# Linear attention followed by a SiLU feed-forward on one Trainium2 core: loads and work units in another order, and query and key transposes by DMA for two thirds of the chunks

## The chip, the cores and the metric

The kernel runs on one core of one Trainium2 chip. Times are microseconds (us) on the device, of the slowest (here the only) core. The span that a profile gives is from the first to the last instruction of the profiled execution and is about 2 us less than the device time of that run.

PE is TensorE (PEld its weight loads, which overlap), DVE is VectorE, ACT is ScalarE, POOL is GpSimd. SP is the SyncE queue, which here issues nearly every DMA, in program order.

## The reference, cut to what matters

```python
# q, k, v: (4 batches, 8 heads, 768 positions, 64), float32; decay lam per head
for b in range(nb):                        # blocks of 64 positions
    intra = einsum(q_b, k_b) * Dmask       # lam ** (i - j) for i >= j, else 0
    out_b = intra @ v_b + (q_b * lam ** (pos + 1)) @ kv_state
    kv_state = lam ** 64 * kv_state + (k_b * lam ** (63 - pos)).T @ v_b
x = out rearranged to (3072 tokens, 512)
h = x @ w_in                               # (512, 2048)
y = (h * sigmoid(h)) @ w_out               # (2048, 512)
```

## The kernel before

It takes 24 chunks of 128 positions (six for each of four batches), all eight heads at once. For each chunk: three loads of 256 KB (q, k, v), scaling of q and k to bf16 on POOL (`prep`), eight TensorE transposes that DVE copies out of psum, the memory that matmuls write to (`st_t`), a state product (`st_d`), scores times the causal mask (`st_s`), and the output, which already comes out transposed for the feed-forward (`st_o`). Queries go to a block-diagonal tile `qbd`, whose other half is zero, so that two heads share a matmul. Chunks are put together to groups of 512 or 256 tokens. A group then has 16 up-projections (`ffn1`, four matmuls each, SiLU on ACT) and, for each chunk, four down-projection units (`ffn2`, four matmuls each).

The program order on each engine is the order in which these functions are called. The parts that matter here:

```python
GROUPS = [512, 256, 256, 512, 512, 512, 512]

def prep(c):
    ...
    nc.gpsimd.tensor_tensor(qb, qf, lam_fwd[...], op=AL.mult)
    nc.gpsimd.tensor_tensor(kb, kf, lam_bwd[...], op=AL.mult)
    nc.scalar.activation(vb, vf, AF.Copy)          # the value cast

def st_t(c):
    tp = psum.tile([128, 2, NP, BLK], BF16, tag="att", bufs=3)
    for p in range(NP):
        nc.tensor.transpose(tp[:, 0, p, :], pair_of(qb, p), ident)
    for p in range(NP):
        nc.tensor.transpose(tp[:, 1, p, :], pair_of(kb, p), ident)
    nc.vector.tensor_copy(qt[0:64, :, 0, :], tp[0:64, 0, :, :])
    nc.vector.tensor_copy(qt[64:128, :, 1, :], tp[64:128, 0, :, :])
    nc.vector.tensor_copy(kt, tp[:, 1, :, :])
...
# start: four chunks, then the first group's up-projections
for c in range(1, n0):
    if c + 1 < n0:
        prep(c + 1)
    st_t(c), st_d(c)
    st_o(c - 1)
    st_s(c)
st_o(n0 - 1)
cast_w("in", 0)
...
for m in range(16):
    ffn1(0, m)
    ...                                            # casts and loads of weights
for i in range(4):
    cast_w("out", i)                               # four casts on DVE, in a row
...
for g in range(1, len(GROUPS)):
    while done_c < cst[g] + nch[g]:                # one attention piece,
        next_att()                                 # one down-projection unit
        next_down(g)
    for m in range(16):
        ffn1(g, m)
        next_down(g)
        ...                                        # attention pieces of the next group
```

## Time and profile before

The time is 257.65 us (median of 4 runs, 256.52 to 258.14).

From the page of the profile, in order: the span; busy time of each engine, its share and its instructions; and three rows with one digit for each of 40 equal slices of the span (6.4 us each): busy tenths of TensorE, granted TensorE clock in tenths (the part of full speed that the throttle allowed), busy tenths of the 16 DMA engines.

```profile
span 254.6 us, 3566 instructions
...
PE 221.1 (87%) x1353; PEld 124.9 (49%) x1376; DVE 102.0 (40%) x177; ACT 112.9 (44%) x238; POOL 51.1 (20%) x57
...
PE   0756994269998899899998999998999999999994
...
PEclk9999999559999999999999999999999999999998
DMA  6999899999999766945397011101101110111122
```

TensorE is at 9 nearly everywhere from slice 9 on, but there is a dip in slices 6 to 8 (38 to 57 us), where the clock falls too, and a slow start up to slice 3 (25 us).

Busy time flatters TensorE, because matmuls overlap. A better measure is pure work: the number of weight loads in a stretch (there is one for each matmul, and none is missing from the trace) times the time from one matmul's start to the next in dense places. Read from the timeline at full clock: 0.216 us for 512 columns (4 in 0.86), 0.163 for 384 (4 in 0.65), 0.109 for 256, 0.056 for a transpose or another 128-column matmul. What a stretch is longer than its work, TensorE lost. This "lost time" is used all through this text.

| stretch, us | work | lost |
|---|---|---|
| 0 to 23.5 | 7.2 | 16.3 |
| 23.5 to 48.5 | 16.7 | 8.3 |
| 48.5 to 80 | 23.5 | 8.0 |
| 80 to 100 | 18.7 | 1.3 |
| 100 to 180 | 76.0 | 4.0 |
| 180 to 254.6 | 69.5 | 5.1 |
| sum | 211.5 | 43.1 |

Three of these stretches in the windows view. The columns are the window, its length, then busy us (and instructions) of PE, PEld, DVE, ACT and POOL, the granted clock, the DMA share and GB/s. (The DMA share is the time that packets took over 16 engines; it goes above 1 where they overlap.)

```profile
23.50:48.50 25.00, 18.30 (x89) 8.11 (x88) 8.02 (x8) 13.41 (x23) 4.17 (x4) 0.93 0.97 296
48.50:80.00 31.50, 25.89 (x172) 16.60 (x176) 15.04 (x27) 10.78 (x28) 9.73 (x10) 0.84 1.17 231
...
100.00:180.00 80.00, 76.93 (x494) 44.03 (x501) 36.56 (x68) 43.23 (x93) 21.83 (x21) 1.00 0.44 89
```

The clock of 0.93 and 0.84 in the first two rows is part of their loss. The Trainium skill ("TensorE: Matmul & The Clock Gate", Part 1) says that TensorE falls to half its clock after an idle window of about 3.4 us and needs as much sustained activity to come back. The trace agrees on the fall and roughly on the return: after the gaps shown next (5.3 and 4.8 us), the four 512-column matmuls at 53.99 us start 0.43 us apart, twice 0.216, full pace is back at about 58.5 us, some 5 us after work resumed at 53.16, and the mean clock from 50 to 60 us is 0.58.

The hole itself, in the timeline view (start, duration, engine, line, operation, output and inputs, count, and in brackets the idle time just before it and what ended that):

```profile
40.74 0.38 PE L173 MATMUL kv_ps<-vb,kb 128*128 128x128 bf16 x4
...
45.17 1.23 DVE L112 CAST w_out_bf<-t 128x2048 bf16<-128x2048 f32 x1 [9.41 <-DMA t<-in_moe_w_out_dram]
46.45 1.86 PE L235 MATMUL o_ps<-w_out_bf,g 128*128 128x512 bf16 x4 [5.33 <-DVE w_out_bf L112]
...
50.67 1.23 DVE L112 CAST w_out_bf<-t 128x2048 bf16<-128x2048 f32 x1 [1.57 <-DMA t<-in_moe_w_out_dram]
...
51.81 0.41 DVE L159 COPY qbd_101<-tp 64x512 bf16<-64x512 bf16 x1
...
53.16 1.03 PE L186 MATMUL sp<-qbd_101,kt 128*128 128x256 bf16 x4 [4.84 <-DVE kt L161]
```

TensorE finishes chunk 4's state product at 41.1 us and then has almost nothing. DVE waits 9.4 us for the second out-weight, casts three out-weights one after another as they come, and only then, at 51.81, copies chunk 4's transposes, which had been in psum since 40 us. So chunk 4's scores start at 53.16.

The transposes, in the groups view (count, busy us and mean ns of one, idle before and what ended it). Keys have a second group of the same size:

```profile
L154 PE MATMUL tp<-ident,qb 128*128 128x128 bf16 x96 | 9.7, 227 | 8.3 <-POOL qb L142 6.8 <-DVE ss L189 1.6
```

A transpose lasts 227 ns, but the next starts 56 ns later, so the 192 of them are 10.7 us of TensorE's work.

### The profile page before, as it was taken

The numbers are of one execution on the slowest core, as the hardware profiler recorded it, in microseconds if no ns is written. First come the engines' busy times: TensorE is split into PE (matmuls) and PEld (weight loads), VectorE is DVE, ScalarE is ACT, GpSimd is POOL, SyncE is SP. The second block draws the span as 40 slices with busy tenths as digits, with TensorE's granted clock in tenths as the row PEclk, the third lists the DMA queues.
The fourth block names the chain that finished last, engine by engine and source line by source line (L and its number), as shares of the span: only waits on it lengthen the run. The fifth ranks groups of instructions, "written<-read, shape, count | busy, mean of one in ns | idle before, by whom it ended". The sixth has DMA issues, their size and how long they took to land.

```text
span 254.6 us, 3566 instructions
## 1 busy us (share of the span) xinstructions
PE 221.1 (87%) x1353; PEld 124.9 (49%) x1376; DVE 102.0 (40%) x177; ACT 112.9 (44%) x238; POOL 51.1 (20%) x57
## 2 busy tenths in 40 slices
PE   0756994269998899899998999998999999999994
PEld 0534442035567667555565555554555544444441
DVE  2678410464345457434463534453353430111221
ACT  4146774003428455736585356535535543333000
POOL 3650033063113333331242231132000000000000
PEclk9999999559999999999999999999999999999998
DMA  6999899999999766945397011101101110111122
GB/s 132 220 259 374 290 232 290 337 221 217 195 269 272 164 148 140 221 74 127 84 230 138 0 41 45 41 1 44 41 0 44 41 41 0 44 41 41 41 85 82
DMA packets 82721, 33.79 MB, mean 133 GB/s; under 512 B 75536, under 2 KB 75536, under 8 KB 82704
## 3 DMA queue, kind: packets, MB, share of 16 engines
q1 hardware_dynamic: 82560, 33.56, 56.3%
q8 instruction: 11, 0.18, 0.3%
q14 instruction: 6, 0.05, 0.1%
q10 hardware_dynamic: 144, 0.00, 0.0%
HBM read 27.27 MB, written 6.29 MB: 132 GB/s over the span
## 4 chain that ended last, share of the span: by engine, by line
PE 73%; DVE 7%; DMA 6%; ACT 5%; SPq 5%; issue 2%; POOL 1%
PE o_ps L235 32%; PE hp L221 25%; DMA t<-in_moe_w_out_dram 5%; PE sp L186 4%; PE op L206 3%; PE op L209 3%; PE tp L156 2%; DVE ss L189 2%; SPq L133 2%; ACT xt L212 2%; PE tp L154 2%; ACT xt L211 2%; PE kv_ps L173 2%; SPq L132 1%; DMA lam_sb<-in_lam_dram 1%
## 5 line engine op out<-in xcount | busy, mean ns | idle before, releaser
L221 PE MATMUL hp<-xt,w_in_bf 128*128 128x512 bf16 (+1 forms) x433 | 98.0, 347 | 6.0 <-ACT xt L212 3.4
L235 PE MATMUL o_ps<-w_out_bf,g 128*128 128x512 bf16 x376 | 96.4, 385 | 5.9 <-DVE w_out_bf L112 5.3
L224 ACT ACTIVATE g<-hp 128x512 bf16<-128x512 f32 (+1 forms) x112 | 59.7, 537 | 80.1 <-PE hp L221 78.4
L235 PEld LDWEIGHTS <-g 128*128 128x128 bf16 x384 | 38.0, 99 | 46.9 <-issue 7.1
L221 PEld LDWEIGHTS <-w_in_bf 128*128 128x128 bf16 x448 | 42.4, 98 | 37.0 <-issue 7.7
L142 POOL TENSOR_TENSOR qb<-qf,lam_fwd 128x512 bf16<-128x512 f32 x24 | 25.0, 1044 | 113.8 <-PE tp L154 76.0
L189 DVE TENSOR_TENSOR ss<-sp,mask 128x512 bf16<-128x512 f32 x48 | 31.1, 686 | 21.4 <-PE sp L186 21.2
L239 DVE COPY ob<-o_ps 128x512 f32<-128x512 f32 x24 | 16.6, 692 | 53.0 <-PE o_ps L235 53.0
L211 ACT ACTIVATE xt<-op 64x256 bf16<-64x256 f32 x48 | 18.1, 377 | 31.6 <-PE op L209 29.4
L143 POOL TENSOR_TENSOR kb<-kf,lam_bwd 128x512 bf16<-128x512 f32 x24 | 25.0, 1043 | 12.7 <-PE kv_ps L173 10.5
L206 PE MATMUL op<-ss,vb 128*128 128x256 bf16 x96 | 22.4, 284 | 0.9 <-DVE ss L189 0.6
L144 ACT ACTIVATE vb<-vf 128x512 bf16<-128x512 f32 x24 | 15.0, 625 | 9.1 <-DMA vf<-in_v_dram 9.0
L212 ACT ACTIVATE xt<-op 64x256 bf16<-64x256 f32 x48 | 18.2, 380 | 0.6
L154 PE MATMUL tp<-ident,qb 128*128 128x128 bf16 x96 | 9.7, 227 | 8.3 <-POOL qb L142 6.8
L186 PEld LDWEIGHTS <-kt 128*128 128x128 bf16 x96 | 9.1, 101 | 16.0 <-DVE kt L161 9.6
L176 DVE CAST kvs<-kv_ps 128x512 bf16<-128x512 f32 x20 | 13.7, 687 | 6.2 <-PE kv_ps L173 6.2
L154 PEld LDWEIGHTS <-qb 128*128 128x128 bf16 x96 | 7.6, 101 | 12.9 <-POOL qb L142 6.7
L206 PEld LDWEIGHTS <-vb 128*128 128x128 bf16 x96 | 9.7, 102 | 4.5 <-DVE ss L189 0.9
L159 DVE COPY qbd_99<-tp 64x512 bf16<-64x512 bf16 x8 | 3.3, 416 | 19.7 <-PE tp L156 19.7
L112 DVE CAST w_out_bf<-t 128x2048 bf16<-128x2048 f32 x4 | 4.9, 1227 | 15.4 <-DMA t<-in_moe_w_out_dram 15.4
L186 PE MATMUL sp<-qbd_101,kt 128*128 128x256 bf16 x32 | 5.6, 298 | 5.7 <-DVE kt L161 4.8
L161 DVE COPY kt<-tp 128x512 bf16<-128x512 bf16 x24 | 10.2, 425 | 0.3
(36 smaller groups left out, 98.3 us busy)
## 6 DMA issues: line engine op xcount, KB each, us to landing
qf<-in_q_dram SPq DMA_DIRECT2D x24, 256.0 KB, 4.9
kf<-in_k_dram SPq DMA_DIRECT2D x24, 256.0 KB, 5.0
vf<-in_v_dram SPq DMA_DIRECT2D x24, 256.0 KB, 5.0
out_dram<-ob SPq DMA_DIRECT2D x24, 256.0 KB, 2.0
t<-in_moe_w_in_dram SPq DMA_DIRECT2D x4, 1024.0 KB, 8.5
t<-in_moe_w_out_dram SPq DMA_DIRECT2D x4, 1024.0 KB, 9.0
lam_sb<-in_lam_dram ACTq DMA_DIRECT2D x1, 4.0 KB, 3.0
```

What stands on the lines that cost most here:

```text
L142: nc.gpsimd.tensor_tensor(qb, qf, lam_fwd[:, blk, :][:, :, None].to_broadcast([128, H, D]), op=AL.mult)
L143: nc.gpsimd.tensor_tensor(kb, kf, lam_bwd[:, blk, :][:, :, None].to_broadcast([128, H, D]), op=AL.mult)
L154: nc.tensor.transpose(tp[:, 0, p, :], pair_of(qb, p), ident)
L186: nc.tensor.matmul(sp[:, 2 * j:2 * j + 2, :], lhsT=kt[:, p, :], rhs=qt[:, p, :, :], start=True, stop=True)
L189: nc.vector.tensor_tensor(ss, sp, mask[:, None, :].to_broadcast([128, 4, BLK]), op=AL.mult)
L206: nc.tensor.matmul(op[:, j, :, :], lhsT=pair_of(vb, p), rhs=res[half][:, 2 * j:2 * j + 2, :], start=True, stop=(blk == 0))
L211: nc.scalar.activation(xt[g][0:64, 2 * half:2 * half + 2, csl], op[0:64, :, 0, :], AF.Copy)
L212: nc.scalar.activation(xt[g][64:128, 2 * half:2 * half + 2, csl], op[64:128, :, 1, :], AF.Copy)
L221: nc.tensor.matmul(hp[:, :n], lhsT=w_in_bf[:, ko, m * 128:(m + 1) * 128], rhs=xt[g][:, ko, :], start=(ko == 0), stop=(ko == KO_IN - 1))
L224: nc.scalar.activation(gg, hp[:, :n], AF.Silu)
L235: nc.tensor.matmul(o, lhsT=gt[g, ko][:, mt * BLK:(mt + 1) * BLK], rhs=w_out_bf[:, ko, :], start=(ko == 0), stop=(ko == KO_OUT - 1))
L239: nc.vector.tensor_copy(ob, o)
```

## The change

The intent is twofold. The first part puts loads, casts and work units in the order in which data come: small first pieces of the in-weights, the first group's evacuations shared between ACT and DVE, up-projections of half the first group before chunk 3 is out, chunks 4 and 5 inside the first group's up-projections, and afterwards stretches in which up-projections, attention pieces and down-projections are merged evenly; the later groups become 384, except the last. An early SiLU also brings ACT's table load forward, from 25.3 to 5.7 us. The second part takes the transposes of chunks 8 to 23 off TensorE: POOL writes the scaled queries into a zero-padded tile, and a DMA transpose makes the block-diagonal tile from it directly.

```diff
-GROUPS = [512, 256, 256, 512, 512, 512, 512]
+GROUPS = [512, 256, 256, 384, 384, 384, 384, 512]
+NPET = 8
...
+    for i in range(NQBD):
+        t = const.tile([128, NP, 4, D], BF16, name=f"qpad{i}")
+        nc.gpsimd.memset(t, 0.0)
+        qpad.append(t)
...
+    W_IN = [(0, 256), (256, 512), (512, 1024), (1024, 1536), (1536, 2048)]
...
     def prep(c):
+        if c < NPET:
+            ...                                     # as before
+        else:
+            qb = qpad[c % NQBD]
+            nc.gpsimd.tensor_tensor(qb[:, :, 0:4:3, :], ..., op=AL.mult)
-        nc.scalar.activation(vb, vf, AF.Copy)
+        vraw[c] = vf                                # cast later, by vcast
...
+    def dma_t(c):
+        qb, kb, vb = natb[c]
+        nc.sync.dma_start_transpose(qt.rearrange("d p j s -> d (p j) s"), qb.rearrange("s p x d -> s (p x d)"))
+        nc.sync.dma_start_transpose(kt, kb.rearrange("s h d -> s (h d)"))
...
+    for c in range(4):
+        load_c(c)
+    for i in range(5):
+        load_w("in", i)
+        if i == 3:
+            load_c(4)
+    load_c(5)
+    load_w("out", 0)
+    for c in range(4):
+        prep(c)
+        st_t(c)
+        if c > 0:
+            st_o(c - 1)
+        if c == 3:
+            cast_w("in", 0)
+        st_s(c), st_d(c)                            # st_d starts with vcast(c)
+    cast_w("in", 1)
+    ffn1(0, 0, 0), ffn1(0, 1, 0)                    # first half of the group
+    st_o(3)
+    ffn1(0, 0, 1), ffn1(0, 1, 1)
...
+    cast_w("in", 4)
+    for m in range(8, 12):
+        ffn1(0, m)
+        if m == 10:
+            st_t(4)
+    load_w("out", 3)
+    prep(5)
+    st_s(4), st_d(4)
+    ffn1(0, 12)
+    ffn1(0, 13)
+    st_o(4)
+    ffn1(0, 14)
+    st_t(5)
+    ffn1(0, 15)
+    cast_w("out", 0)
+    st_s(5), st_d(5)
+    ffn2(0, 0, range(0, 4))
+    st_o(5)
+    ffn2(0, 1, range(0, 4))
...
+    for g in range(2, len(GROUPS)):
+        parts = [(ups(g), 0, 1), (pieces(g + 1), 0, 0.85)]
+        if g > 2:
+            parts.append((downs(g - 1, range(nch[g - 1])), 0, 1))
+        stretch(*parts)                             # merged by position
```

More of the change, by code (lines that the diff above doesn't have):

```diff
@@ L44 @@
     wpool = ctx.enter_context(tc.tile_pool(name="wpool", bufs=1))
-    wio = ctx.enter_context(tc.tile_pool(name="wio", bufs=3))
-    io = ctx.enter_context(tc.tile_pool(name="io", bufs=7))
-    nat = ctx.enter_context(tc.tile_pool(name="nat", bufs=3))
+    wio = ctx.enter_context(tc.tile_pool(name="wio", bufs=4))
+    io = ctx.enter_context(tc.tile_pool(name="io", bufs=6))
+    nat = ctx.enter_context(tc.tile_pool(name="nat", bufs=4))
     work = ctx.enter_context(tc.tile_pool(name="work", bufs=4))
@@ L74 @@
     NQBD = 3
-    qbd = []
+    qbd, qpad = [], []
     for i in range(NQBD):
@@ L95 @@
     nc.scalar.activation(lam_bwd, lam_exp, AF.Exp, scale=-1.0)
+    warm = const.tile([128, 1], F32)
+    nc.scalar.activation(warm, mask[:, 0:1], AF.Silu)
     w_in_bf = wpool.tile([128, KO_IN, DFF], BF16)
@@ L102 @@
     wtmp = {}
+    W_IN = [(0, 256), (256, 512), (512, 1024), (1024, 1536), (1536, 2048)]
+    W_OUT = [(0, 4), (4, 8), (8, 12), (12, 16)]
     def load_w(which, i):
-        t = wio.tile([128, 4, 512], F32, tag="w_tmp")
-        src = w_in_r[:, :, i * 512:(i + 1) * 512] if which == "in" else w_out_r[:, i * 4:(i + 1) * 4, :]
+        small = which == "in" and i < 2
+        t = wio.tile([128, 1024 if small else 2048], F32, name="w_tmp", tag="w_small" if small else "w_tmp",
+                     bufs=2 if small else 4)
+        if which == "in":
+            a, z = W_IN[i]
+            t = t.rearrange("p (ko f) -> p ko f", ko=4)
+            src = w_in_r[:, :, a:z]
+        else:
+            a, z = W_OUT[i]
+            t = t.rearrange("p (ko f) -> p ko f", ko=4)
+            src = w_out_r[:, a:z, :]
         nc.sync.dma_start(out=t, in_=src)
@@ L110, in cast_w @@
     def cast_w(which, i):
-        dst = w_in_bf[:, :, i * 512:(i + 1) * 512] if which == "in" else w_out_bf[:, i * 4:(i + 1) * 4, :]
-        nc.vector.tensor_copy(dst, wtmp.pop((which, i)))
+        t = wtmp.pop((which, i))
+        if which == "in":
+            a, z = W_IN[i]
+            dst = w_in_bf[:, :, a:z]
+        else:
+            a, z = W_OUT[i]
+            dst = w_out_bf[:, a:z, :]
+        if which == "in" and i < 2:
+            nc.vector.tensor_copy(dst[:, 0:2, :], t[:, 0:2, :])
+            nc.scalar.activation(dst[:, 2:4, :], t[:, 2:4, :], AF.Copy)
+        else:
+            nc.vector.tensor_copy(dst, t)
     raw, natb, tr, st, kvb, kvps = {}, {}, {}, {}, {}, {}
@@ L138, in prep, with vcast @@
         qf, kf, vf = raw.pop(c)
-        qb = nat.tile([128, H, D], BF16, tag="qb")
+        if c < NPET:
+            qb = nat.tile([128, H, D], BF16, tag="qb")
+            nc.gpsimd.tensor_tensor(qb, qf, lam_fwd[:, blk, :][:, :, None].to_broadcast([128, H, D]), op=AL.mult)
+        else:
+            qb = qpad[c % NQBD]
+            nc.gpsimd.tensor_tensor(
+                qb[:, :, 0:4:3, :], qf.rearrange("s (p j) d -> s p j d", j=2),
+                lam_fwd[:, blk, :].rearrange("s (p j) -> s p j", j=2)[:, :, :, None].to_broadcast([128, NP, 2, D]),
+                op=AL.mult)
         kb = nat.tile([128, H, D], BF16, tag="kb")
         vb = nat.tile([128, H, D], BF16, tag="vb")
-        nc.gpsimd.tensor_tensor(qb, qf, lam_fwd[:, blk, :][:, :, None].to_broadcast([128, H, D]), op=AL.mult)
         nc.gpsimd.tensor_tensor(kb, kf, lam_bwd[:, blk, :][:, :, None].to_broadcast([128, H, D]), op=AL.mult)
-        nc.scalar.activation(vb, vf, AF.Copy)
+        vraw[c] = vf
         natb[c] = (qb, kb, vb)
+    vraw = {}
+    def vcast(c):
+        if c in vraw:
+            nc.scalar.activation(natb[c][2], vraw.pop(c), AF.Copy)
+    def dma_t(c):
+        qb, kb, vb = natb[c]
+        kt = work.tile([128, NP, BLK], BF16, tag="kt")
+        qt = nat.tile([128, NP, 2, BLK], BF16, tag="qt")
+        nc.sync.dma_start_transpose(qt.rearrange("d p j s -> d (p j) s"), qb.rearrange("s p x d -> s (p x d)"))
+        nc.sync.dma_start_transpose(kt, kb.rearrange("s h d -> s (h d)"))
+        tr[c] = (qt, kt)
     def pair_of(t, p):
@@ L151, in st_t @@
         qb, kb, vb = natb[c]
-        tp = psum.tile([128, 2, NP, BLK], BF16, tag="att", bufs=3)
+        first = c < GROUPS[0] // BLK
+        tp = psum.tile([128, 2, NP, BLK], BF16, name="tp", tag="o" if first else "att", bufs=2 if first else 3)
         for p in range(NP):
@@ L160, in st_t @@
         nc.vector.tensor_copy(qt[64:128, :, 1, :], tp[64:128, 0, :, :])
-        nc.vector.tensor_copy(kt, tp[:, 1, :, :])
+        if first:
+            nc.scalar.activation(kt, tp[:, 1, :, :], AF.Copy)
+        else:
+            nc.vector.tensor_copy(kt, tp[:, 1, :, :])
         tr[c] = (qt, kt)
@@ L165, in st_d @@
         blk = c % NB
+        qb, kb, vb = natb[c]
+        vcast(c)
         if blk == NB - 1:
             return
-        qb, kb, vb = natb[c]
         if blk == 0:
@@ L175, in st_d @@
         kvs = work.tile([128, NP, BLK], BF16, tag="kvs")
-        nc.vector.tensor_copy(kvs, kv)
+        if c < GROUPS[0] // BLK:
+            nc.scalar.activation(kvs, kv, AF.Copy)
+        else:
+            nc.vector.tensor_copy(kvs, kv)
         kvb[c + 1] = kvs
@@ L210, in st_o, with ffn1 @@
                                      start=False, stop=True)
-            nc.scalar.activation(xt[g][0:64, 2 * half:2 * half + 2, csl], op[0:64, :, 0, :], AF.Copy)
-            nc.scalar.activation(xt[g][64:128, 2 * half:2 * half + 2, csl], op[64:128, :, 1, :], AF.Copy)
+            ps = slice(2 * half, 2 * half + 2)
+            if c < GROUPS[0] // BLK and half == 1:
+                nc.vector.tensor_copy(xt[g][0:64, ps, csl], op[0:64, :, 0, :])
+                nc.vector.tensor_copy(xt[g][64:128, ps, csl], op[64:128, :, 1, :])
+            else:
+                nc.scalar.activation(xt[g][0:64, ps, csl], op[0:64, :, 0, :], AF.Copy)
+                nc.scalar.activation(xt[g][64:128, ps, csl], op[64:128, :, 1, :], AF.Copy)
     gt = {}
-    def ffn1(g, m):
+    hps = {}
+    def ffn1(g, m, part=None):
         n = GROUPS[g]
-        hp = psum.tile([128, 512], F32, tag="h", bufs=2)
+        a, z = (0, n) if part is None else (part * n // 2, (part + 1) * n // 2)
+        if a == 0:
+            hps[g, m] = psum.tile([128, 512], F32, name="h_ps", tag="h", bufs=2)
+        hp = hps[g, m]
         for ko in range(KO_IN):
-            nc.tensor.matmul(hp[:, :n], lhsT=w_in_bf[:, ko, m * 128:(m + 1) * 128], rhs=xt[g][:, ko, :],
-                             start=(ko == 0), stop=(ko == KO_IN - 1))
-        gg = gpool.tile([128, n], BF16, name="g", tag="g", padded_shape=[128, 512])
-        nc.scalar.activation(gg, hp[:, :n], AF.Silu)
-        gt[g, m] = gg
+            nc.tensor.matmul(hp[:, a:z], lhsT=w_in_bf[:, ko, m * 128:(m + 1) * 128], rhs=xt[g][:, ko, a:z],
+                             start=(ko == 0 and a == 0), stop=(ko == KO_IN - 1), skip_group_check=True)
+        if z == n:
+            gg = gpool.tile([128, n], BF16, name="g", tag="g", padded_shape=[128, 512])
+            nc.scalar.activation(gg, hp[:, :n], AF.Silu)
+            gt[g, m] = gg
     ops = {}
@@ L245 @@
     cst = [sum(nch[:g]) for g in range(len(GROUPS))]
-    loads = list(range(NCHUNK))
-    for c in range(nch[0]):
-        load_c(loads.pop(0))
-    for i in range(4):
-        if i < 3:
-            load_w("in", i)
-    n0 = nch[0]
-    prep(0)
-    prep(1)
-    st_t(0), st_d(0), st_s(0)
-    for c in range(1, n0):
-        if c + 1 < n0:
-            prep(c + 1)
-        st_t(c), st_d(c)
-        st_o(c - 1)
-        st_s(c)
-    st_o(n0 - 1)
-    cast_w("in", 0)
-    load_w("in", 3)
-    cast_w("in", 1)
@@ L269 @@
-    load_w("out", 0)
-    wseq = [("out", 1), ("out", 2), ("out", 3)]
-    for c in range(2):
-        load_c(loads.pop(0))
-    att = []
-    for c in range(n0, NCHUNK):
-        att += [(c, "t"), (c, "d"), (c, "s"), (c, "o")]
-    fns = {"t": st_t, "d": st_d, "s": st_s, "o": st_o}
-    prepped = n0
-    done_c = n0
-    def next_att():
-        nonlocal prepped, done_c
-        if not att:
-            return
-        c, kind = att.pop(0)
-        while prepped <= min(c + 1, NCHUNK - 1):
-            prep(prepped)
-            prepped += 1
+    for c in range(4):
+        load_c(c)
@@ new lines @@
+    for i in range(5):
[12 more added lines that the diff above has]
+        st_s(c), st_d(c)
+    cast_w("in", 1)
+    ffn1(0, 0, 0), ffn1(0, 1, 0)
+    st_o(3)
+    ffn1(0, 0, 1), ffn1(0, 1, 1)
+    cast_w("in", 2)
+    load_w("out", 1)
+    ffn1(0, 2), ffn1(0, 3)
+    prep(4)
+    cast_w("in", 3)
@@ new lines @@
+    load_w("out", 2)
+    for m in range(4, 8):
+        ffn1(0, m)
+    cast_w("in", 4)
+    for m in range(8, 12):
+        ffn1(0, m)
+        if m == 10:
[14 more added lines that the diff above has]
+    ffn2(0, 1, range(0, 4))
+    load_c(6)
+    load_c(7)
+    loads = list(range(8, NCHUNK))
@@ L290, in next_att, with next_prep, piece @@
+    fns = {"t": st_t, "d": st_d, "s": st_s, "o": st_o}
+    state = {"prepped": 6}
+    def next_prep():
+        c = state["prepped"]
+        if c < NCHUNK:
+            prep(c)
+            if c >= NPET:
+                dma_t(c)
+            state["prepped"] = c + 1
             if loads:
                 load_c(loads.pop(0))
+    def piece(c, kind):
+        while state["prepped"] <= min(c + 2, NCHUNK - 1):
+            next_prep()
         fns[kind](c)
-        if kind == "o":
-            done_c = c + 1
@@ L297 @@
-    for m in range(16):
-        ffn1(0, m)
-        if m == 3:
-            cast_w("in", 2)
-            load_w(*wseq.pop(0))
-        if m == 7:
-            cast_w("in", 3)
-            load_w(*wseq.pop(0))
-        if m == 11:
-            load_w(*wseq.pop(0)) if wseq else None
-    for i in range(4):
-        cast_w("out", i)
-        if wseq:
-            load_w(*wseq.pop(0))
-    while loads and loads[0] < n0 + 6:
-        load_c(loads.pop(0))
-    downs = []
-    for g in range(len(GROUPS)):
-        for mt in range(nch[g]):
-            for kk in range(4):
-                downs.append((g, mt, range(4 * kk, 4 * kk + 4)))
@@ L320, in next_down @@
-    def next_down(limit):
-        if downs and downs[0][0] < limit:
-            ffn2(*downs.pop(0))
-            return True
-        return False
-    for g in range(1, len(GROUPS)):
-        while done_c < cst[g] + nch[g]:
-            next_att()
-            next_down(g)
-        npieces = 4 * (nch[g + 1] if g + 1 < len(GROUPS) else 0)
-        acc = 0.0
-        for m in range(16):
-            ffn1(g, m)
-            left_groups = len(GROUPS) - g
-            next_down(g)
-            acc += npieces / 16.0
-            while acc >= 1.0:
-                next_att()
-                acc -= 1.0
@@ L341, with ups, downs, pieces @@
-    while downs:
-        next_down(len(GROUPS))
+        if kind == "s":
+            vcast(c + 1)
+    def ups(g):
+        return [(ffn1, g, m) for m in range(16)]
+    def downs(g, mts):
+        return [(ffn2, g, mt, range(4 * kk, 4 * kk + 4)) for mt in mts for kk in range(4)]
+    def pieces(g):
+        if g >= len(GROUPS):
+            return []
+        return [(piece, c, kind) for c in range(cst[g], cst[g] + nch[g])
+                for kind in (("t", "d", "s", "o") if c < NPET else ("d", "s", "o"))]
@@ new lines, in stretch @@
+    def stretch(*parts):
+        units = []
+        for i, (items, a, z) in enumerate(parts):
+            units += [(a + (z - a) * (j + 0.5) / len(items), i, j, it) for j, it in enumerate(items)]
+        for _, _, _, (fn, *args) in sorted(units, key=lambda u: u[:3]):
+            fn(*args)
+    early = [(ffn2, 0, mt, range(4 * kk, 4 * kk + 4)) for kk in range(1, 4) for mt in range(2)]
+    casts = [(cast_w, "out", i) for i in range(1, 4)]
+    stretch((ups(1), 0, 1), (casts, 0.0, 0.7), (early, 0.2, 0.9), ([(next_prep,), (next_prep,)], 0.6, 0.8),
+            (downs(0, range(2, 4)), 0.9, 1.3))
@@ L346 @@
+    stretch((downs(1, range(2)), 0, 1), (pieces(2), 0, 0.8))
+    for g in range(2, len(GROUPS)):
[3 more added lines that the diff above has]
+        stretch(*parts)
+    stretch((downs(len(GROUPS) - 1, range(nch[-1])), 0, 1))
 _INS = ['q', 'k', 'v', 'lam', 'moe_w_in', 'moe_w_out']
```

## The prediction

> **What bounds the kernel now.** TensorE, but not everywhere. The page gives it 221 of 254.6 us busy (87%), and the chain of waits is 73% PE. Back-to-back the trace shows 0.216 us per 512-column matmul and about 0.055 us per 128-column transpose. With the counts of the groups view I estimate the PE's pure work: up- and down-projection 83 us each, transposes 10.7, state products 4.5, scores 10.5, outputs 19.2, together about 211 us. So some 44 us of the span are lost. By windows:
> - 0 to 24.8 us: 7.5 us of work, 17 lost. First up-projection at 24.85. The first four chunks run as a serial chain through POOL, PE, DVE and back.
> - 24.8 to 55: 17.5 us of work, 12.7 lost. The timeline shows PE nearly empty from 41 to 53: three out-weight loads queued behind chunk loads, casts on DVE waiting 9.4 us for one; the granted clock falls to 0.58 for 50 to 60 us.
> - 55 to 140: 77 of 85, partly the cold clock.
> - 140 to 236: 94 of 96.
> - Tail about 3 us, unchanged.
>
> **What the change does.**
> 1. Loads in order of need (small first weight pieces; out-weights last), first transposes in another psum pool, up-projection of half the first group before chunk 3 is out. SP issues a chunk load in about 1.13 us and a 1 MB weight in 2.7, so chunk 3 is in at about 17 us whatever the order, first weights at 18.5; I expect up-projections dense from about 20.5 us: gain about 4.
> 2. The hole at 41 to 53 should nearly close: first out-weight lands at about 37 us, when the sixteenth up-projection ends; 2 to 4 us of waits remain, and no cold clock. Gain about 10 to 12 with the clock.
> 3. 16 chunks lose 8 PE transposes each: 128 x 0.055 = 7 us off the PE, all critical in the dense stretch. DVE loses 3 copies (1.27 us) per chunk, 20 us, off the path.
> 4. Added: two DMA transposes per chunk, 256 KB (half of it zeros) and 128 KB. The Trainium skill, "DMA: Bandwidth & Descriptors", section "Latency and other measured facts", gives 261 GB/s effective for DMA transposes: an estimate of 1.5 us per chunk; no run shows it yet. SP then has about 3.3 (loads) + 0.5 (store) + 2 to 4 us of issue per chunk against about 8.3 us of PE work. They are prepared two chunks ahead, so they should hide. DMA share after 140 us is only 0.08.
> 5. Three zero fills on POOL at start: POOL idles 3.6 us before its first product, so free.
>
> **Sum.** Work 203.5; start loss 13; middle 3; steady 4; tail 3.5: span about 227, measured time about 2 to 3 more: 230 us. Range 220 to 247. Faster by over 2%: 0.92; within: 0.05; slower: 0.03.
>
> **What the profile would show.** First up-projection before 22 us; PE slices of 9 from there with no slice under 7; clock never under 0.9 after 25 us; transposes only in 8 chunks; late scores not waiting for a DMA; DVE busy down by about 20 us.
>
> **What would make it wrong.** DMA transposes far slower than the estimate (over some 8 us of SP or DMA time per chunk), so that scores wait for them, or SP stuck on a transpose waiting for POOL while loads and stores queue behind it; ACT, in order, blocking silu behind the value casts moved into it.

## The result

The changed kernel takes 234.97 us (median of 4 runs, 233.95 to 235.67); the ratio to before is 0.912, with a 95% interval of 0.907 to 0.917. Ratios in this text are the mean time of one kernel's runs over that of the other's of the same rounds, so they are not quite the ratio of the quoted medians. Executions over 1.5% slower than the fastest of the same kernel are left out of the means. In a later set of runs on another occasion it took 235.22 us, ratio 0.918.

The same lines of the page, after (slices of 5.8 us):

```profile
span 232.2 us, 3510 instructions
...
PE 209.8 (90%) x1320; PEld 123.5 (53%) x1320; DVE 81.3 (35%) x130; ACT 117.9 (51%) x257; POOL 54.3 (23%) x60
...
PE   0465898899999988999999999999999999999993
...
PEclk9999999999999999999999999999999999999999
DMA  6999999999939998999999997999640100110212
```

The dip and the cold clock are gone, and DVE has 20.7 us less to do. The DMA row is now mostly at 9 up to slice 27 (162 us), where before it was mostly under 8 from slice 14 on and fell to 0 at slice 22 (140 us).

| stretch, us | work before | lost before | work after | lost after |
|---|---|---|---|---|
| 0 to 23.5 | 7.2 | 16.3 | 6.8 | 16.7 |
| 23.5 to 48.5 | 16.7 | 8.3 | 21.2 | 3.8 |
| 48.5 to 80 | 23.5 | 8.0 | 30.5 | 1.0 |
| 80 to 100 | 18.7 | 1.3 | 17.7 | 2.3 |
| 100 to 180 | 76.0 | 4.0 | 80.2 | -0.2 |
| 180 to the end | 69.5 | 5.1 | 48.0 | 4.2 |
| sum | 211.5 | 43.1 | 204.4 | 27.8 |

The span fell by 22.4 us: 7.1 us of work removed and 15.3 us less lost. The 7.1 is a count, not a timing: 128 transposes fewer at 0.056 us each. What they were worth in time, e1_all_tensor and e2_dma_alone tell. The loss fell by 11.5 us between 23.5 and 80 us and by 4.2 between 100 and 180. At the start it did not fall.

```profile
23.50:48.50 25.00, 22.41 (x144) 12.68 (x141) 13.68 (x20) 15.55 (x31) 4.66 (x4) 1.00 1.07 316
48.50:80.00 31.50, 30.93 (x208) 18.92 (x207) 12.34 (x21) 11.44 (x30) 10.39 (x10) 1.00 0.88 196
80.00:100.00 20.00, 18.25 (x145) 13.50 (x144) 6.32 (x11) 15.38 (x39) 6.21 (x6) 1.00 1.02 202
100.00:180.00 80.00, 80.00 (x509) 48.08 (x507) 26.85 (x41) 45.94 (x103) 20.80 (x20) 1.00 0.92 176
```

TensorE is busy for all 80 us of the last row, at full clock and beside a DMA share of 0.92 (0.44 before). In the row from 80 to 100 us ACT is busy for 15.4 of 20.

Where the hole was, the timeline now reads:

```profile
35.20 0.39 PE L209 MATMUL tp<-ident,qb 128*128 128x128 bf16 x4
...
37.22 0.61 PE L248 MATMUL sp<-qbd_101,kt 128*128 128x256 bf16 x4 [0.55 <-DVE kt L219]
...
44.69 1.02 PE L308 MATMUL o_ps<-w_out_bf,g 128*128 128x512 bf16 x4 [0.52 <-DVE w_out_bf L145]
...
47.28 2.39 PE L293 MATMUL h_ps<-xt,w_in_bf 128*128 128x256 bf16 x16
```

Chunk 4's transposes now come inside the up-projections, its scores 2 us after them, and the first down-projection waits 0.52 us for its weight. Note that the first out-weight's cast ends only at 44.6 us; before, the first ended at 35.8 and the second at 46.4. From the issues' landing times, the four out-weights came at 40.6, 43.2, 46.3 and 49.2 us; before, at 34.5, 45.2, 47.9 and 50.7. So the first came 6 us later and the others only 1.4 to 2 us earlier. TensorE got other things to do meanwhile.

The transposes that stayed on TensorE, queries:

```profile
L209 PE MATMUL tp<-ident,qb 128*128 128x128 bf16 x32 | 3.6, 242 | 6.7 <-POOL qb L174 6.7
```

They are a third of what they were. Where the rest went can be seen in SP's queue, one chunk's period (the duration is how long SP was held by the issue):

```profile
108.62 0.57 SPq L164 DMA_DIRECT2D qf<-in_q_dram  x1
109.25 0.57 SPq L165 DMA_DIRECT2D kf<-in_k_dram  x1
109.92 0.91 SPq L166 DMA_DIRECT2D vf<-in_v_dram  x1
110.93 0.85 SPq L314 DMA_DIRECT2D out_dram<-ob  x1
111.89 1.45 SPq L197 DMA_TRANSPOSE qt<-qpad_105  x1
113.42 1.23 SPq L198 DMA_TRANSPOSE kt<-kb  x1
114.70 0.57 SPq L164 DMA_DIRECT2D qf<-in_q_dram  x1
```

From chunk load to chunk load it is 6.1 us here. From 90.2 to 133.7 us there are seven such periods, 6.2 us on average. The issues follow each other with almost no gap.

TensorE in this stretch does not take a chunk every 6.2 us all the time: the scores of chunk 8 start at 79.3 us, of chunk 13 at 107.3, of chunk 23 at 183.8, so 5.6 us per chunk first, 7.7 later, and 7.0 over all fifteen periods. The transposes run ahead of it. At the tightest (chunk 11) the keys' transpose lands at 91.3 us, 3.2 us before its scores at 94.5.

### The profile page after: what moved, and what is told of

It is laid out like the page before. It is cut to its first block, busy times and chain, and to the rows that moved or that the text cites. A ratio compares the mean times of both kernels' runs of the same rounds, so it can differ in the third digit from the quotient of the medians.

```text
span 232.2 us, 3510 instructions
## 1 busy us (share of the span) xinstructions
PE 209.8 (90%) x1320; PEld 123.5 (53%) x1320; DVE 81.3 (35%) x130; ACT 117.9 (51%) x257; POOL 54.3 (23%) x60
## 3 DMA queue, kind: packets, MB, share of 16 engines
q1 hardware_dynamic: 108688, 39.86, 77.4%
## 4 chain that ended last, share of the span: by engine, by line
PE 83%; ACT 7%; DVE 5%; issue 2%; DMA 1%; POOL 1%; ACTq 0%
PE o_ps L308 35%; PE h_ps L293 34%; PE sp L248 4%; PE op L268 4%; PE op L271 3%; PE kv_ps L232 2%; ACT xt L279 2%; ACT xt L278 2%; DMA lam_sb<-in_lam_dram 1%; ACT vb L191 1%; ACT kt L217 1%; PE tp L211 1%; ACT g L297 1%; DVE ss L251 1%; PE tp L209 1%
## 5 line engine op out<-in xcount | busy, mean ns | idle before, releaser
L293 PE MATMUL h_ps<-xt,w_in_bf 128*128 128x384 bf16 (+2 forms) x520 | 98.9, 323 | 2.6 <-ACT g L297 1.9
L297 ACT ACTIVATE g<-h_ps 128x384 bf16<-128x384 f32 (+2 forms) x128 | 62.3, 490 | 69.1 <-PE h_ps L293 68.2
L293 PEld LDWEIGHTS <-w_in_bf 128*128 128x128 bf16 x520 | 50.3, 98 | 37.4 <-issue 3.9
L278 ACT ACTIVATE xt<-op 64x256 bf16<-64x256 f32 x44 | 16.5, 375 | 17.8 <-PE op L271 8.7
L268 PE MATMUL op<-ss,vb 128*128 128x256 bf16 x96 | 21.6, 277 | 0.2
L238 DVE CAST kvs<-kv_ps 128x512 bf16<-128x512 f32 x16 | 11.0, 688 | 24.7 <-PE kv_ps L232 24.7
L279 ACT ACTIVATE xt<-op 64x256 bf16<-64x256 f32 x44 | 16.6, 378 | 0.5
L174 POOL TENSOR_TENSOR qb<-qf,lam_fwd 128x512 bf16<-128x512 f32 x8 | 8.9, 1109 | 33.7 <-DMA qf<-in_q_dram 32.8
L248 PEld LDWEIGHTS <-kt 128*128 128x128 bf16 x96 | 8.8, 99 | 11.5 <-ACT kt L217 5.3
L271 PE MATMUL op<-qt,kvs 128*128 128x256 bf16 x56 | 13.1, 272 | 0.0
L177 POOL TENSOR_TENSOR qpad_107<-qf,lam_fwd 128x512 bf16<-128x512 f32 x5 | 5.2, 1042 | 27.1 <-DMA qf<-in_q_dram 23.3
L177 POOL TENSOR_TENSOR qpad_109<-qf,lam_fwd 128x512 bf16<-128x512 f32 x6 | 6.3, 1042 | 20.0 <-DMA qf<-in_q_dram 12.6
L177 POOL TENSOR_TENSOR qpad_105<-qf,lam_fwd 128x512 bf16<-128x512 f32 x5 | 5.2, 1042 | 22.4 <-DMA qf<-in_q_dram 19.4
L232 PE MATMUL kv_ps<-vb,kb 128*128 128x128 bf16 x80 | 8.0, 223 | 2.6 <-ACT vb L191 2.6
L209 PE MATMUL tp<-ident,qb 128*128 128x128 bf16 x32 | 3.6, 242 | 6.7 <-POOL qb L174 6.7
```

The lines of the kernel that those rows point to most:

```text
L177: nc.gpsimd.tensor_tensor(qb[:, :, 0:4:3, :], qf.rearrange("s (p j) d -> s p j d", j=2), lam_fwd[:, blk, :].rearrange("s (p j) -> s p j", ...
L248: nc.tensor.matmul(sp[:, 2 * j:2 * j + 2, :], lhsT=kt[:, p, :], rhs=qt[:, p, :, :], start=True, stop=True)
L268: nc.tensor.matmul(op[:, j, :, :], lhsT=pair_of(vb, p), rhs=res[half][:, 2 * j:2 * j + 2, :], start=True, stop=(blk == 0))
L271: nc.tensor.matmul(op[:, j, :, :], lhsT=kvb[c][:, p, :], rhs=qt[:, p, :, :], start=False, stop=True)
L278: nc.scalar.activation(xt[g][0:64, ps, csl], op[0:64, :, 0, :], AF.Copy)
L279: nc.scalar.activation(xt[g][64:128, ps, csl], op[64:128, :, 1, :], AF.Copy)
```

## The experiments

Twelve runs were made, in four sets on four chips; each set has its own runs of the kernel before (medians 256.2 to 257.0 us), and a ratio compares within its set. The two halves of the change were separated first, then the reasons inside each.

| kernel | us, median | ratio to before | lost to 48.5 us |
|---|---|---|---|
| changed, control (c1_changed) | 235.22 | 0.918 | 21.4 |
| changed, all transposes on TensorE (e1_all_tensor) | 244.40 | 0.952 | 22.9 |
| before, with DMA transposes (e2_dma_alone) | 249.67 | 0.971 | 25.0 |
| changed, DMA transposes doubled (e3_double) | 258.77 | 1.009 | 21.6 |
| changed, chunks 4 and 5 late again (e5_late_attn) | 248.35 | 0.967 | 26.6 |
| changed, chunks 4 and 5 loaded later (e6_late_chunks) | 235.32 | 0.917 | 21.4 |
| before, casts just in time (e7_before_lazy) | 255.01 | 0.993 | 24.6 |
| changed, early value casts (e8_early_v) | 233.32 | 0.914 | 21.6 |
| changed, DVE helps ACT (e9_act_relief) | 232.83 | 0.909 | 21.2 |
| changed, wide loads, wrong results (e10_wide) | 236.08 | 0.922 | 22.1 |
| reordered (b1_reordered) | 232.86 | 0.908 | 21.5 |
| reordered, wide loads, wrong results (w1_reordered_wide) | 234.41 | 0.913 | 22.7 |

The control is the changed kernel itself:

> The changed kernel again, unaltered, as the control for the three that follow on the same chip: 0.912 of before, 234 to 236 us.

The time came out as expected; the ratio is a little higher (interval 0.914 to 0.923). Two of its six runs had full clock and took 234.6 us; the profiled one, at 235.15, had a clock of 0.57 between 24 and 28 us.

### What the DMA transposes gave: the two halves apart

The changed kernel with all transposes on TensorE, everything else kept:

```diff
-NPET = 8
+NPET = 24
```

> The changed kernel with every chunk transposed on TensorE (no DMA transposes), the new order kept. Theory 'the transposes were critical PE work': 16 chunks x 8 transposes x 0.056 us = 7.2 us come back and nothing else, about 242 us, ratio to before about 0.94. Rival 'the DMA transposes cost something back elsewhere (DMA share 1.0 from 80 to 150 us)': less than 4 us slower. Second rival 'the psum and DVE round trip of a TensorE transpose costs more than its PE time': over 10 us slower.

It took 244.40 us, 9.2 us more than the control's median. Of this 7.2 us is work, by the count of its transposes. Its loss from 100 to 180 us is 0.2, so the other half, the new order and its groups of 384, not the DMA transposes, removed the 4.0 that the kernel before lost there. The other 2 us are not explained. They are not the dip in the clock after 24 us that its profiled run shows: the control's has it too, and among runs at full clock the difference is the same (243.8 against 234.6). The rival that the DMA gives something back falls. The result lies between the plain theory (7.2) and the second rival, that the round trip through psum and DVE costs more (over 10); a weaker form of that rival is not excluded.

The opposite edit, the DMA transposes added to the kernel before and nothing else:

```diff
+        if c >= NPET: qb = qpad[c % NQBD]; ...      # prep, as in the change
+            if prepped >= NPET:
+                dma_t(prepped)
-        att += [(c, "t"), (c, "d"), (c, "s"), (c, "o")]
+        att += [(c, kind) for kind in (("t", "d", "s", "o") if c < NPET else ("d", "s", "o"))]
```

> The kernel before with the DMA transposes from the ninth chunk on as its only change (zero-padded tiles, transposes issued one chunk ahead as its products are). If the two halves of the change are independent: 7 us off, about 250.5 us, ratio 0.972. If the late issue (one chunk ahead) or the DMA queue full until about 110 us makes scores wait for the transposes: 255 us or more.

It took 249.67 us, ratio 0.971: 6.5 us by the medians, 7.4 by the ratio, whose interval (0.964 to 0.978) leaves 6 to 9 us. The two halves are close to independent: the transposes are worth 7 to 9 us, the order about 12 (244.40 against 256.21).

### How near the DMA is to its limit

```diff
         nc.sync.dma_start_transpose(kt, kb.rearrange("s h d -> s (h d)"))
+        nc.sync.dma_start_transpose(qt2.rearrange(...), qb.rearrange(...))   # scratch tiles
+        nc.sync.dma_start_transpose(kt2, kb.rearrange("s h d -> s (h d)"))
```

> The changed kernel with each of its 32 DMA transposes issued twice, the second into a scratch tile that nobody reads (36 instead of 40 buffers for the activations to make room). If the transposes hide with room to spare: no change, 235 us. If the DMA queue is nearly full while they run (its share reads 1.0 from 80 to 150 us, and they land only some 3 to 5 us before their scores): scores wait for DMA, 8 us or more slower, with the losses between 70 and 170 us.

It took 258.77 us, 24 us more, and slower than the kernel before. One chunk's period of SP's queue:

```profile
110.83 0.58 SPq L164 DMA_DIRECT2D qf<-in_q_dram  x1
...
113.00 3.41 SPq L197 DMA_TRANSPOSE qt<-qpad  x1
116.50 1.22 SPq L198 DMA_TRANSPOSE kt<-kb  x1
117.81 1.26 SPq L201 DMA_TRANSPOSE qt<-qpad  x1
119.12 1.27 SPq L202 DMA_TRANSPOSE kt<-kb  x1
120.44 0.58 SPq L164 DMA_DIRECT2D qf<-in_q_dram  x1
```

From chunk load to chunk load it is 9.6 us here, and 9.07 on average over ten periods (84.67 to 175.40 us). An estimate of TensorE's work per chunk in the groups of 384 is 8.5 us: for three chunks 64 x 0.163 of up-projections, 48 x 0.216 of down-projections and 3 x 1.53 of attention. But the first of these chunks are made beside a group of 256 and the last four beside a single group of three chunks, so over chunks 8 to 23 the changed kernel took one every 7.0 us. Behind these 7.0 the 6.2 us of DMA issue fit; 9.07 do not. In the doubled kernel the same scores run from 80.9 to 208.0 us, 8.5 us per chunk (less than 9.07, because the first transposes ran ahead): 22.6 us more than in the changed one, nearly the whole loss of 24. Its last chunk's first transpose is issued at 203 us instead of 168, and in the waits view (who waited for whom: us in total, times, longest) a line is there that the changed kernel does not have:

```profile
PE sp L252 <- DMA kt<-kb: 18.0, 7, 3.4
```

So the transposes are hidden, but with less than 1 us per chunk to spare on average. (The doubled kernel also has 36 in place of 40 activation buffers; that was not tried alone.) Whether SP's issue or the 16 DMA engines set the 9.07 us is not separated: both are full (DMA share 0.97 to 1.04 from 75 to 200 us).

This also gives the price of a transpose. From the queue line of the page, the packets of the main queue took 77.4% of 232.2 us in the changed kernel and 58.1% of 243.4 with all transposes on TensorE: 38.3 us, or 2.4 us of all 16 engines for each chunk's 384 KB. The same difference for e2_dma_alone against before is 2.2 us, for e3_double against the changed kernel 2.2 us. That is 165 to 180 GB/s, where the Trainium skill ("DMA: Bandwidth & Descriptors", section "Latency and other measured facts") gives 261 with a non-contiguous middle dimension, and more for the contiguous case. The prediction took the 261 without this condition; no run shows which case these transposes are. Here they run beside loads, and packets that overlap count twice, so part of this time may be sharing.

### Why the hole closed: order of units, not of loads

```diff
-        if m == 10:
-            st_t(4)
 ...
+    for m in range(12, 16):
+        ffn1(0, m)
+    for i in range(4):
+        cast_w("out", i)
+    st_t(4)
+    st_s(4), st_d(4)
+    st_o(4)
+    st_t(5)
+    st_s(5), st_d(5)
```

> The changed kernel with one piece of the old order back: the four casts of the out-weights on DVE, and after them chunks 4 and 5 of the attention, all behind the last up-projection of the first group. Theory 'the hole of before was DVE order: chunk copies behind casts that wait for out-weights': hole of some 8 us returns between 40 and 50 us, about 242 us. Rival 'the hole closed because loads come in another order': under 2 us slower.

It took 248.35 us, 13 us more; the whole order is worth about 12. The hole is back, with the same signature: four casts on DVE that wait for their weights, and chunk 4's scores behind them.

```profile
40.89 1.23 DVE L145 CAST w_out_bf<-w_tmp 128x2048 bf16<-128x2048 f32 x1 [5.35 <-DMA w_tmp<-in_moe_w_out_dram]
...
49.40 1.23 DVE L145 CAST w_out_bf<-w_tmp 128x2048 bf16<-128x2048 f32 x1 [1.57 <-DMA w_tmp<-in_moe_w_out_dram]
...
52.01 1.03 PE L248 MATMUL sp<-qbd,kt 128*128 128x256 bf16 x4 [10.15 <-DVE kt L219]
```

Lost time is 9.6 us from 23.5 to 48.5 and 7.2 from 48.5 to 80 (control 4.5 and 1.3). This moves the chunks on TensorE and on DVE together. The order of the loads alone:

```diff
     for i in range(5):
         load_w("in", i)
-        if i == 3:
-            load_c(4)
-    load_c(5)
     load_w("out", 0)
+    load_c(4)
+    load_c(5)
```

> The changed kernel with the old order of loads in one respect: all in-weights and the first out-weight ahead of chunks 4 and 5 (before: chunk 4 after the in-weights and the first out-weight). If the order of loads closed the hole: chunk 4 comes about 5 us later, its transposes, emitted inside the first group's up-projections, hold TensorE up, 4 us or more slower. If the order of units on TensorE and DVE did: under 2 us.

It took 235.32 us: no change. This part of the load order does not matter. Nor does an earlier arrival: in e10_wide, below, the out-weights land at 31.6 to 40.7 us instead of 40.6 to 49.2, and the loss up to 48.5 us is no smaller. Then the cure of DVE's order alone, in the kernel before:

```diff
+        if ("out", kos[0] // 4) in wtmp:            # in ffn2, ahead of its matmuls
+            cast_w("out", kos[0] // 4)
-    for i in range(4):
-        cast_w("out", i)
```

> The kernel before with one change: each cast of an out-weight is emitted just ahead of the first down-projection that needs it, instead of all four ahead of chunks 4 and 5. The late-attention run put those casts back into the changed kernel and lost about 13 us. If DVE order alone makes the hole, most of it goes here too: 6 to 10 us off, about 248. But TensorE takes its units in order, and a down-projection of the second out-weight (in at 45 us) stands ahead of chunk 4's outputs there: then only 2 to 4 us off.

It took 255.01 us, 1.5 us less by the medians. The hole stays (7.3 us lost from 23.5 to 48.5, 5.7 from 48.5 to 80, so 13.0 after 16.3), because TensorE too takes its units in order: in its trace the down-projections at 47.24 and 52.04 us wait for the second and third out-weight's casts, and chunk 4's outputs stand behind them.

```profile
47.24 1.86 PE L237 MATMUL o_ps<-w_out_bf,g 128*128 128x512 bf16 x4 [1.91 <-DVE w_out_bf L112]
...
52.04 1.02 PE L237 MATMUL o_ps<-w_out_bf,g 128*128 128x512 bf16 x4 [2.09 <-DVE w_out_bf L112]
```

So curing DVE's order is not enough; the changed kernel has the chunks ahead of the late weights on both engines. The opposite test, TensorE's order cured alone, was not made.

### The start

In the changed kernel the first up-projection starts at 23.51 us, against 24.85 before. Such times differ between executions: it is 23.5 to 24.2 us in five profiles with the same start (after, c1_changed, e3_double, e5_late_attn, e9_act_relief), and 26.43 in e7_before_lazy, which has the start of before. The timeline gives two reasons to test. The first three lines are the scores of chunks 1 and 2 and chunk 2's state product, the last the first up-projection, which stands right behind chunk 3's state product:

```profile
13.92 0.61 PE L248 MATMUL sp<-qbd_101,kt 128*128 128x256 bf16 x4 [0.91 <-ACT kt L217]
...
17.69 0.61 PE L248 MATMUL sp<-qbd_103,kt 128*128 128x256 bf16 x4 [0.77 <-ACT kt L217]
...
19.00 0.38 PE L232 MATMUL kv_ps<-vb,kb 128*128 128x128 bf16 x4 [0.69 <-ACT vb L191]
...
23.51 1.04 PE L293 MATMUL h_ps<-xt,w_in_bf 128*128 128x256 bf16 x8
```

Scores come 3.77 us apart. The state product waits for a value cast that ACT does late in its own order, and chunk 3's transposes stand behind it. The chunk loads take 3.5 us per chunk as well. To see which it is, the loads were made fast, at the price of wrong results:

```diff
-        nc.sync.dma_start(out=qf, in_=q[b, :, sl, :].rearrange("h s d -> s h d"))
+        for tf, src in ((qf, q), (kf, k), (vf, v)):
+            rows = src.rearrange("b h (t x) d -> (b h t) x d", x=8)
+            nc.sync.dma_start(out=tf, in_=rows[c * 128:(c + 1) * 128])
```

> Wrong results on purpose: the changed kernel with each query, key and value load taking 128 rows of 2 KB contiguous (other rows of the same arrays) in place of 1024 rows of 256 B, the same bytes. Theory 'the start and the stretch to 48 us are bound by the rate of the 256-byte chunk loads (about 1.13 us per 256 KB)': chunks come in less than 0.9 us per load, first up-projection before 21.5 us, the out-weights in by 45 us, 4 us or more off in all. Rival 'the start is bound by the chain POOL, TensorE, DVE, ACT per chunk (3.77 us from chunk to chunk)': first up-projection stays at 23 to 23.5 us, under 2 us off.

The last of the twelve loads is issued at 7.0 us instead of 13.0, and the four chunks' values land 2.0 us apart, from 6.3 to 12.4 us instead of 7.3 to 18.0. Yet the scores of chunks 0 to 3 still come 3.8 to 4.4 us apart (11.04, 14.99, 19.38 and 23.17), and the first up-projection starts later than in the control:

```profile
7.01 0.33 SPq L166 DMA_DIRECT2D vf<-in_v_dram  x1
...
25.21 1.04 PE L293 MATMUL h_ps<-xt,w_in_bf 128*128 128x256 bf16 x8
```

The time is 236.08 us. So the loads do not bound the start; what is left is the chain from engine to engine. (The start is even 1.7 us later. 1.1 of it is the small load of lam, which landed at 4.82 us instead of 3.74, beside the faster traffic, so that the first decay factors were late; the rest is within the spread of equal starts.)

Then the value casts ahead of their state products:

```diff
         natb[c] = (qb, kb, vb)
+        if c < GROUPS[0] // BLK:
+            vcast(c)
```

> The changed kernel with the value casts of the first four chunks on ACT right after their products, as in the kernel before, in place of just ahead of the state product. In the changed kernel's trace chunk 3's transposes stand behind chunk 2's state product, which waits 0.7 us for that cast, and the first up-projection stands behind chunk 3's, which waits 1.2. If those waits set the start: first up-projection about 1.5 us earlier (22 us), 1 to 1.5 us off in all. If the stretch to 48 us is limited by what the DMA has brought: the start moves but the end does not, under 0.5 us. If ACT then waits for the value loads ahead of more urgent work: slower.

The first up-projection moves to 21.08 us, 2.4 us earlier, and the median is 233.32 us, 1.9 less than the control. The interval of its ratio (0.908 to 0.920) overlaps the control's (0.914 to 0.923). Among runs with a granted clock of at least 0.998, four of it lie at 233.0 to 233.4 and two of the control at 234.6, so about 1.4 us stays. (b1_reordered, with the same early casts, starts at 22.35, only 1.2 us earlier.) The profiled run is one of the two with a clock dip, here between 36 and 44 us, so part of its loss there is the clock. Where more of it goes, its timeline shows:

```profile
21.08 0.38 PE L295 MATMUL h_ps<-xt,w_in_bf 128*128 128x256 bf16 x2
...
34.72 1.23 DVE L145 CAST w_in_bf<-w_tmp 128x2048 bf16<-128x2048 f32 x1 [5.18 <-DMA w_tmp<-in_moe_w_in_dram]
...
37.35 0.65 PE L250 MATMUL sp<-qbd,kt 128*128 128x256 bf16 x4 [2.68 <-DVE kt L221]
```

The last in-weight's cast waits 5.18 us for its DMA, and DVE has chunk 4's copies in order behind it, so the scores come at 37.35.

### The stretch from 80 to 100 us

Group 2 has 256 tokens while the three chunks of group 3 are made, so ACT has as many SiLU calls and more evacuations for less TensorE work.

```diff
-            if c < GROUPS[0] // BLK and half == 1:
+            if (c < GROUPS[0] // BLK or 8 <= c < 11) and half == 1:
                 nc.vector.tensor_copy(xt[g][0:64, ps, csl], op[0:64, :, 0, :])
```

> The changed kernel with the second half of the attention output of chunks 8, 9 and 10 evacuated by DVE (busy 1.4 to 5 of 10 us there) in place of ACT (busy 8.5 of 10). Theory 'the 2.2 us lost between 80 and 100 us are up-projections waiting for ACT to empty their psum': 1 to 2 us off, and the waits of the up-projections for the silu of 1.6 us gone. Rival 'they are attention latency': no change.

It took 232.83 us (six runs, 232.0 to 234.0; control 234.6 to 236.1, so no run of the one reaches the other, though the intervals of the ratios just overlap). The windows view of 80 to 100 us, first the control:

```profile
80.00:100.00 20.00, 18.18 (x147) 13.86 (x146) 7.40 (x12) 15.29 (x39) 6.26 (x6) 1.00 1.01 201
```

and with the help of DVE:

```profile
80.00:100.00 20.00, 19.38 (x154) 14.35 (x154) 10.11 (x18) 14.11 (x35) 6.25 (x6) 1.00 1.11 208
```

ACT gives 1.2 us to DVE, TensorE gains 1.2 us of busy time, and the loss in this window falls from 2.2 to 1.0 us. The time that up-projections wait for a SiLU falls from 1.9 us in the control to 0.2. The first theory holds.

### An attempt at a version better than both

```diff
+        if c < GROUPS[0] // BLK: vcast(c)                      # as e8_early_v
+            if (c < GROUPS[0] // BLK or 8 <= c < 11) ...       # as e9_act_relief
-    cast_w("in", 4)
     for m in range(8, 12):
         ffn1(0, m)
-        if m == 10:
+        if m == 9:
             st_t(4)
+    st_s(4), st_d(4)
+    cast_w("in", 4)
+    load_w("out", 3)
+    prep(5)
+    st_o(4)
 ...                       # first down-projections and their cast after st_o(5)
```

> An attempt at a better kernel: the changed one with the value casts of the first four chunks early, the second half of chunks 8 to 10 evacuated by DVE, and chunks 4 and 5 moved so that their DVE copies come ahead of the cast of the last in-weight (which waits 5 us for its DMA) and no down-projection stands ahead of chunk 5's outputs. The early-value run started 2.4 us sooner and gave that back between 34 and 37 us behind that cast. If that reading holds: 2 us or more below the better of the two single edits (233), about 230, loss between 23.5 and 48.5 us down from 4.5 to under 3 us. If the stretch is bound by the DMA itself: no better than 232.

It took 232.86 us: much better than before, but no better than the single edit for ACT. The window from 80 to 100 loses 0.4 us and the start 16.0, but 23.5 to 48.5 loses 5.4: the reading behind the reordering failed. In its trace chunk 4's state product waits for a value cast on ACT, and the last in-weight's cast, now behind chunk 4 on DVE, holds up the up-projections for 1.34 us. To see whether the loads limit this stretch once the start is shorter, the wide loads were put on top:

```diff
-        nc.sync.dma_start(out=qf, in_=q[b, :, sl, :].rearrange("h s d -> s h d"))
+        for tf, src in ((qf, q), (kf, k), (vf, v)):            # as e10_wide, in the reordered kernel
```

> Wrong results on purpose: the reordered kernel with the wide loads (2 KB rows, same bytes). In five kernels that differ in their start, the loss up to 48.5 us came out at 20.4 to 21.6 us, and 22.1 with wide loads alone. Two limits could stand behind each other: the chain per chunk at the start, and the arrival of the chunk loads and in-weights after it. If they do, the reordering alone gave nothing, the wide loads alone gave nothing, and both together give 2 us or more: loss up to 48.5 us under 19, about 230 us. If something else (DVE and ACT order in that stretch) sets it: loss stays at 21, no better than 232.5.

It took 234.41 us and lost 22.7 us up to 48.5. The loads are not the limit here either. The waits in its trace are the same ones, for the value cast (0.77 us) and for the weight cast (1.11 us). What an arrangement of ACT and DVE that fits would give in this stretch stays open: ten profiles that keep the new order of units (all of the changed and reordered kernels but e5_late_attn) lost between 20.5 and 22.9 us up to 48.5 us.

Not tried alone: groups of 384 against 512, the small first weight pieces, the half-group up-projections, the first group's evacuations shared with ACT, the early SiLU table load, the buffer counts, and DMA transposes without the zero padding.

## Why the prediction was right, and where its sum was off

The time (235.0 predicted as 230, range 220 to 247) and the direction were right. Of what the profile was to show, all came but one (TensorE's slices are 8s and 9s): the first up-projection was not before 22 us. Point by point:

- The removed TensorE work: 7 us predicted, 7.1 by the count in the two traces; in time 6.5 to 7.4 us in e2_dma_alone and 9.2 in e1_all_tensor. Right, with some 2 us of the latter unexplained.
- DVE down by about 20 us: 20.7. Transposes by DMA hidden: right, no score waits for a DMA in the changed kernel. The reason given for it was too easy. The prediction took 1.5 us per chunk from 261 GB/s and pointed at a DMA share of 0.08 after 140 us. The transposes cost 2.2 to 2.4 us of all engines, and the share became 0.92 from 100 to 180 us. It set 8.3 us of TensorE work per chunk against them; TensorE took a chunk every 7.0 us. The slack is 0.8 us per chunk (7.0 minus 6.2), and e3_double (9.07) went through it.
- The hole: predicted 2 to 4 us of loss after the first up-projections, 3.8 measured, and no cold clock. Right in size, wrong in its mechanism, so the size was partly luck. It says that the first out-weight "lands at about 37 us"; it landed at 40.6 and its cast ended at 44.6. The order of the loads, which the prediction credits, is worth nothing as far as e6_late_chunks tests it; the order of units on TensorE and DVE is worth the gain (e5_late_attn, e7_before_lazy).
- The start is the step that failed: "chunk 3 is in at about 17 us whatever the order, first weights at 18.5; I expect up-projections dense from about 20.5 us: gain about 4". The first started at 23.51 us, and the loss up to there was 16.7 us instead of the 13 in the sum; against before (16.3) nothing was gained. The step priced the arrival of the data. These came 1.0 us later than it says (chunk 3's values landed at 18.0, the first weights at 19.5), at most a third of the 3.0 us by which the start came late. What binds is the chain per chunk from POOL to TensorE, DVE, ACT and back, 3.77 us from chunk to chunk; with the four chunks' loads all issued by 7.3 us (e10_wide) the start is no earlier. This term alone is 3.7 of the 5.2 us by which the span (232.2) exceeds the predicted 227.
- Steady state: 4 us predicted as lost, 3.6 measured after 48.5 us without the tail (1.0 + 2.3 - 0.2 + 0.5). But 2.3 of them are a new loss between 80 and 100 us, ACT at 15.4 of 20, which the prediction named only as a danger from value casts. It is evacuations beside SiLU (e9_act_relief).

## What to carry to other kernels

Here work that was taken off a dense engine paid in full, because the path that took it over had slack; measure the slack by doubling the added work, because busy shares averaged over the span hide it, and so does the work per unit of one typical stretch. When an engine idles behind a late load, look first at what stands in order behind that wait on every in-order engine: here moving the loads changed nothing where it was tried, and curing DVE's queue left TensorE waiting in its own order. And price a pipeline's start by its period from engine to engine, not by the arrival of its data.

## What the Trainium skill lacked or had wrong

- "DMA: Bandwidth & Descriptors", section "Latency and other measured facts": 261 GB/s for a DMA transpose with a non-contiguous middle dimension, more for a contiguous one. Here SBUF-to-SBUF transposes of 256 and 128 KB beside other traffic cost 2.2 to 2.4 us of all 16 engines per 384 KB, 165 to 180 GB/s (an estimate from the queue's packet time, which includes overlap).
- The same page, "DMA Transpose (X-bar)", gives no time from issue to landing for a small transpose. Here the median was 4.1 to 4.5 us for 256 KB and 2.9 us for 128 KB, and each held SP for at least 1.2 us.
- "TensorE: Matmul & The Clock Gate", Part 4, gives 275 to 390 ns for a 128x128 transpose. That is a latency. In this trace one lasts 227 ns, but the next starts 56 ns later, and e2_dma_alone saved 51 to 58 ns for each of 128 transposes removed.
